# Three zero matmuls instead of one as fillers in each of the first twelve attention steps

## The chip, the cores and the metric

The kernel runs on one core of one Trainium2 chip. The metric is the device time of one execution in microseconds (us). In what follows PE is TensorE, DVE VectorE, ACT ScalarE, POOL GpSimd and SP SyncE, which issues the DMAs.

## The reference

The reference is a local attention followed by a gated layer. The batch is 4, there are 8 heads, 768 positions and 64 channels a head. A query sees the first 8 keys of the sequence (the global ones) and the 96 keys up to its own.

```python
scores = scale * np.matmul(q, k.transpose(0, 1, 3, 2))
...
scores = scores + bias[None, :, :, :]
scores = np.where(keep, scores, -1000000000.0)
scores = scores - np.max(scores, axis=-1, keepdims=True)
a = np.exp(scores)
a = a / (np.sum(a, axis=-1, keepdims=True) + 1e-09)
return np.matmul(a, v).astype(np.float32)
...
for k in range(K):
    gate_pre += conv_w[k][None, None, :] * xp[:, k:k + S, :]
gate = 1.0 / (1.0 + np.exp(-gate_pre))
val = x @ w_val
return (gate * val @ w_out).astype(np.float32)
```

The attention output x (512 channels) goes through a causal convolution of five taps, whose sigmoid gates the product of x with w_val. The gated value is multiplied with w_out.

## The kernel before

The work is cut into 32 groups (batch, half of the sequence, pair of heads), each of three steps, so 96 steps of 128 queries by two heads. What a step does, and on which engine:

- S (L406, PE): for a whole group at once, the scores of its three steps, twelve matmuls into four PSUM banks. The banks of one group are the only ones, so S of the next group waits until all bias passes of this one have read them.
- AM (L414, DVE): the bias pass, one for each head. It adds the bias to the scores, scales, and keeps the row minimum in `mins`. Tile t.
- EX (L424, ACT): the exponential with its sum `sm`. Then `sm` is guarded (L431, POOL or DVE), its reciprocal `rs` taken (L434, DVE) and the probabilities p multiplied by it (L439, POOL or DVE, two instructions a step).
- PT (L449, L452, L455, PE): transposes of p into the bank `pt`, of which there is one. EV (L149 on ACT, L151 on DVE) copies it to `a`.
- PV (L473, L477, L480, PE): once a group, the product with v into the bank `x`, of which there is one. Before it, four columns of history are put there (L548 a memset, or a copy).
- From x come xh (a rounded copy, L149 or L151), xl (the rest, L556, DVE) and the five taps of the convolution (the first L566 on ACT or L568 on DVE, the other four L564 on DVE). The bank is free for the next group when these are done.

Four groups make a phase, of which there are eight. For each phase a sigmoid on ACT (L599, with a table load before it and one behind it), 48 matmuls `val` (L606), the gating g = val times gate (L613, DVE), its split into gh and gl (L619, POOL or DVE), and 36 matmuls `o` (L626), whose result is copied (`ob`) and stored. The two banks of `val` and `o` take turns, so the second `o` of a phase waits for the g of the fourth `val`. The fourth `val` of phase 0 is val_0_3, its gated value g_0_3, its second output o_0_1.

At the start eight blocks of 64-bit weights, ('w', 0) to ('w', 7), are taken apart: an absolute value on ACT (L305), five passes on DVE (L313 to L325), a rounded copy (L149 on ACT or L151 on DVE) and two passes for the rest (L344, L348, POOL or DVE). The first four become wvh and wvl, the others woh and wol.

The order of the instructions on each engine is fixed when the program is built. Each operation is added to `Plan` with a due time, the engines that may do it and an assumed cost on each, and the operations that it follows. `Plan.order` (L80) goes through them as a list scheduler: it takes the engine that could start something first, and of what could start there, what is due first; where an operation may run on two engines, it takes the one that would end it first. A changed cost of one operation therefore moves others, on every engine. At run time each engine goes through its own list strictly in that order and waits by semaphores for data alone.

The fillers are matmuls of ones by ones, 128x512 in bfloat16, into the tile `warm` (`zeros`, L235 to L242), of which nothing is read. Eight stand at the program's start. One more operation F for each of the twelve steps of the first four groups (L245 to L248) issues `FILL_N` of them. In the plan F follows the bias pass of its step, but it reads nothing of that pass, so that on the chip it waits for nothing except its place in PE's list.

Of the kernel before, what the change touches and what calls it, by code (L numbers as in the profile page):

```python
# [16 lines left out]
WARM = 8  # L17
S_B, PT_B, X_B = 4, 1, 1
U_D1, RAW_B = -0.4, 4
FILL_N, FILL_TO, U_F = 1, 4, 0.2  # L20
W_AT = (0, 3, 6, 9, 14.5, 17, 22, 22.5)
SPARE = {"vector": 0.6, "gpsimd": -0.2, "scalar": 0.0}
XH_B, GATE_B, P_B, T_B, A_B, V_B, W_B, WT_B = 7, 2, 5, 8, 9, 4, 2, 1
# [874 lines left out]
```

## Time and profile before

| | us |
|---|---|
| three runs | 317.21, 318.02, 318.74 |
| median | 318.02 |
| the profiled execution, its time | 317.56 |
| its span, first to last instruction | 315.8 |
| PE busy in the span | 282.6 |
| DVE busy in the span | 230.2 |
| mean granted PE clock | 0.966 |

The profiled execution is 0.46 us below the median, and 1.76 us of its time lie outside the span. Times in the profile count from the span's start. A row of the list of instructions has the start, the duration, the engine and line, the operation, the tile written and those read, and in brackets the engine's idle time before it and what ended it. Durations of neighbours overlap by some 0.07 us, since an instruction starts before the one ahead has drained. A row of a table by stretches has the stretch, its length, and the busy time of each engine with its instructions. The granted clock is a share of TensorE's full clock.

### The profile page before, as it was taken

The numbers are of one execution on the slowest core, as the hardware profiler recorded it, in microseconds if no ns is written. First come the engines' busy times: TensorE is split into PE (matmuls) and PEld (weight loads), VectorE is DVE, ScalarE is ACT, GpSimd is POOL, SyncE is SP. The second block draws the span as 40 slices with busy tenths as digits, with TensorE's granted clock in tenths as the row PEclk, the third lists the DMA queues.
The fourth block names the chain that finished last, engine by engine and source line by source line (L and its number), as shares of the span: only waits on it lengthen the run. The fifth ranks groups of instructions, "written<-read, shape, count | busy, mean of one in ns | idle before, by whom it ended". The sixth has DMA issues, their size and how long they took to land.

```text
span 315.8 us, 6866 instructions
## 1 busy us (share of the span) xinstructions
PE 282.6 (89%) x2131; PEld 225.6 (71%) x2133; DVE 230.2 (73%) x807; ACT 230.0 (73%) x643; POOL 159.2 (50%) x338
## 2 busy tenths in 40 slices
PE   7487766697999999999999999999999999999992
PEld 2254555585788778887787777888788777888981
DVE  5899889999679676787766777978676767885410
ACT  2667677977789677977797769977895779785320
POOL 5977968586335353355426443554434542750220
PEclk9769799989999999999999999999999999999997
DMA  6768655203444435332450444323443221001102
GB/s 188 267 220 258 190 172 180 85 2 85 125 138 137 120 109 179 117 86 73 137 175 26 118 138 141 119 86 92 155 147 92 67 84 70 0 3 61 41 36 75
DMA packets 21069, 36.27 MB, mean 115 GB/s; under 512 B 2592, under 2 KB 12832, under 8 KB 21024
## 3 DMA queue, kind: packets, MB, share of 16 engines
q1 hardware_dynamic: 21024, 35.75, 36.4%
q8 instruction: 19, 0.31, 0.4%
q14 instruction: 26, 0.21, 0.2%
HBM read 29.45 MB, written 6.29 MB: 113 GB/s over the span
## 4 chain that ended last, share of the span: by engine, by line
PE 40%; DVE 29%; POOL 10%; ACT 8%; issue 5%; DMA 4%; SPq 1%; POOLq 0%; ACTq 0%
PE o L626 13%; DVE gate L564 12%; PE val L606 9%; DVE t L414 7%; POOL p L439 6%; PE x L477 5%; PE x L480 3%; DVE xl L556 3%; PE s L406 3%; PE pt L452 3%; ACT gate L566 3%; PE pt L455 2%; POOL sm L431 2%; ACT p L424 2%; DMA v<-in_v 2%
## 5 line engine op out<-in xcount | busy, mean ns | idle before, releaser
L424 ACT ACTIVATE p<-t,mins 128x232 f32<-128x232 f32 (+1 forms) x192 | 90.3, 472 | 22.2 <-DVE mins L414 17.1
L439 POOL TENSOR_SCALAR p<-p,rs 128x232 f32<-128x232 f32 (+1 forms) x179 | 84.9, 487 | 33.3 <-DVE rs L434 22.9
L564 DVE SCALAR_TENSOR_TENSOR gate<-x,cwt,gate 128x384 f32<-128x384 f32 x128 | 78.1, 610 | 7.8 <-ACT gate L566 7.4
L414 DVE CUSTOM_DVE_ANT_0 t<-s,bias 128x232 f32<-128x232 f32 (+1 forms) x192 | 67.4, 371 | 0.0
L431 POOL TENSOR_SCALAR sm<-sm 128x2 f32<-128x2 f32 x92 | 20.8, 226 | 84.6 <-ACT p L424 79.5
L149 ACT COPY a<-pt 128x464 f32<-128x464 f32 (+1 forms) x90 | 46.2, 513 | 18.5 <-PE pt L455 13.7
L606 PE MATMUL val<-xh,wvh 128*128 128x384 f32 x128 | 48.0, 375 | 2.5 <-DVE g L613 2.2
L406 PE MATMUL s<-rk,rq 64*128 64x232 f32 (+1 forms) x384 | 44.9, 360 | 4.0 <-DVE ('w', 0)_y L313 2.8
L606 PE MATMUL val<-xl,wvh 128*128 128x384 f32 x128 | 44.2, 346 | 1.2 <-DVE xl L556 1.2
L626 PE MATMUL o<-woh,gh 128*128 128x512 f32 x96 | 41.4, 432 | 3.3 <-DVE g L613 3.3
L606 PE MATMUL val<-xh,wvl 128*128 128x384 f32 x128 | 44.2, 346 | 0.0
L452 PE MATMUL pt<-ident,p 104*128 104x104 f32 x160 | 33.2, 276 | 11.7 <-ACT a L149 5.2
L452 PEld LDWEIGHTS pt<-ident,p 104*128 104x128 f32 x160 | 19.6, 141 | 31.9 <-POOL p L439 16.9
L434 DVE RECIPROCAL rs<-sm 128x2 f32<-128x2 f32 x96 | 15.6, 162 | 34.6 <-POOL sm L431 33.3
L406 PEld LDWEIGHTS s<-rk,rq 64*128 64x128 f32 x384 | 32.4, 186 | 11.2 <-DVE ('w', 0)_y L313 3.3
L626 PE MATMUL o<-wol,gh 128*128 128x512 f32 x96 | 37.9, 395 | 0.0
L626 PE MATMUL o<-woh,gl 128*128 128x512 f32 x96 | 37.8, 394 | 0.0
L424 ACT ACTIVATION_READ_ACCUMULATOR p<-t,mins 128x1 f32 x192 | 36.4, 190 | 0.0
L619 POOL TENSOR_TENSOR gl<-g,gh 128x384 fp32r<-128x384 f32 x27 | 27.7, 1026 | 16.3 <-ACT gh L149 15.1
L477 PE MATMUL x<-a,v 128*64 128x128 f32 x320 | 32.5, 281 | 0.3 <-ACT a L149 0.2
L455 PE MATMUL pt<-ident,p 128*128 128x128 f32 x160 | 31.4, 278 | 0.0
L606 PEld LDWEIGHTS val<-xh,wvh 128*128 128x128 f32 x128 | 24.8, 194 | 5.2 <-DVE g L613 3.8
(150 smaller groups left out, 465.9 us busy)
## 6 DMA issues: line engine op xcount, KB each, us to landing
rq<-in_qT SPq DMA_DIRECT2D x32, 192.0 KB, 3.6
v<-in_vw SPq DMA_DIRECT2D x16, 384.0 KB, 3.2
out<-ob SPq DMA_DIRECT2D x24, 256.0 KB, 2.1
v<-in_vw SPq DMA_DIRECT2D x16, 256.0 KB, 2.8
rk<-in_kT SPq DMA_DIRECT2D x16, 252.0 KB, 3.7
rk<-in_kT SPq DMA_DIRECT2D x16, 200.0 KB, 3.1
w<-in_wv SPq DMA_DIRECT2D x4, 512.0 KB, 4.6
w<-in_wo SPq DMA_DIRECT2D x4, 512.0 KB, 4.5
```

Source lines behind the costliest of these rows:

```text
L149: nc.scalar.copy(dst, src)
L406: nc.tensor.matmul(T["s", g, k, j][:, :n], T["rq", g][r, k * P : (k + 1) * P], T["rk", g][r, c0 : c0 + n], start=True, stop=True)
L414: nc.vector.tensor_tensor_reduce(out=t[:, :n], in0=T["s", s // HB, s % HB, j][:, :n], in1=bias[:, h, :P] if n == P else bias[:, h, P:], op ...
L424: nc.scalar.activation(T["p", s][:, j, :n], T["t", s, j][:, :n], AF.Exp, bias=mins[:, s, j : j + 1], scale=-1.0, accum_out=T["sm", s][:, j ...
L439: engine(e).tensor_scalar(out=pr, in0=pr, scalar1=rs, scalar2=1.0, op0=ALU.mult, op1=ALU.mult)
L452: nc.tensor.transpose(pt[:, j * QA : (j + 1) * QA], pr[:QA, j, :P], ident[:QA, :QA])
L455: nc.tensor.transpose(pt[:, c : c + P], pr[:, j, CA:], ident)
L477: nc.tensor.matmul(head(j, P), T["v", g][:, k, j, 1], a[:, 2 * QA + j * P : 2 * QA + (j + 1) * P], start=True, stop=False)
L564: nc.vector.scalar_tensor_tensor(out=gt, in0=src, scalar=w, in1=gt, op0=ALU.mult, op1=ALU.add)
L606: nc.tensor.matmul(T["val", ph, m], (wvh, wvh, wvl)[r][:, c, m * P : (m + 1) * P], (T["xh", g], T["xl", g], T["xh", g])[r], start=(c == 0 ...
L619: engine(e).tensor_sub(tile_of(("gl", ph, m), [P, HT], F32R, "gl", 5), T["g", ph, m], T["gh", ph, m])
L626: nc.tensor.matmul(T["o", ph, k], (T["gh", ph, c], T["gl", ph, c], T["gh", ph, c])[r][:, cols], (woh, woh, wol)[r][:, c], start=(c == 0 an ...
```

## The change

One number changes:

```diff
-FILL_N, FILL_TO, U_F = 1, 4, 0.2
+FILL_N, FILL_TO, U_F = 3, 4, 0.2
```

Each of the twelve F operations now issues three of the matmuls, 24 more in all. Its cost in the plan is `0.22 * FILL_N` and goes from 0.22 to 0.66 us, so the list scheduler sets the operations of the first groups in another order, on all engines. From PV of group 6 and the scores of group 8 on, the lists of both programs are the same. The listings below show three places ahead of that where they differ. A listing gives line, instruction, tile written and read, and size; the last number of a name is only the buffer's.

On PE, behind the transposes of step 5 (first row), before: the fillers, the scores of group 3, the transposes of step 6 and then PV of group 1.

```order
L455 MATMUL pt_405<-ident,p_338 128x128 x2
L239 LDWEIGHTS const-bfloat16-1.0
L239 MATMUL warm<-const-bfloat16-1.0 128x512
...
L406 MATMUL s_0_456<-rk_268,rq_276 128x128
...
L406 MATMUL s_3_459<-rk_268,rq_276 128x232
L449 MATMUL pt_480<-ident,p_400 128x128 x2
L473 MATMUL x_469<-a_347,v_1_151 64x128 x2
...
L480 MATMUL x_469<-a_423,v_158 64x104 x2
```

The same place now:

```order
L455 MATMUL pt_418<-ident,p_343 128x128 x2
L239 LDWEIGHTS const-bfloat16-1.0
L239 MATMUL warm<-const-bfloat16-1.0 128x512
...
L473 MATMUL x_464<-a_356,v_1_151 64x128 x2
...
L480 MATMUL x_464<-a_432,v_158 64x104 x2
L449 MATMUL pt_492<-ident,p_423 128x128 x2
...
L406 MATMUL s_0_513<-rk_274,rq_282 128x128
...
L406 MATMUL s_3_516<-rk_274,rq_282 128x232
```

PV of group 1 and the transposes of step 6 have moved ahead of the scores of group 3; the three fillers ahead of the scores are now six ahead of PV and three between step 6 and the scores.

On POOL, from the first rest pass of weight block 6 on, before. Here sm_877 is step 17, sm_908 step 18, sm_926 step 19 and sm_938 step 20.

```order
L344 TENSOR_TENSOR ('w', 6)_h<-('w', 6)_h,woh 128x512
L431 TENSOR_SCALAR sm_877<-sm_877 128x2
L348 TENSOR_TENSOR wol<-('w', 6)_h,('w', 6)_r 128x512
L439 TENSOR_SCALAR p_876<-p_876,rs_921 128x232 x2
L431 TENSOR_SCALAR sm_908<-sm_908 128x2
L431 TENSOR_SCALAR sm_926<-sm_926 128x2
L439 TENSOR_SCALAR p_907<-p_907,rs_950 128x232 x2
L431 TENSOR_SCALAR sm_938<-sm_938 128x2
L439 TENSOR_SCALAR p_937<-p_937,rs_978 128x232 x2
L619 TENSOR_TENSOR gl_2_1005<-g_2_940,gh_2_981 128x384
L344 TENSOR_TENSOR ('w', 7)_h<-('w', 7)_h,woh 128x512
L348 TENSOR_TENSOR wol<-('w', 7)_h,('w', 7)_r 128x512
```

And now, where sm_826 is step 16, sm_887 step 17, sm_913 step 18 and sm_932 step 19:

```order
L344 TENSOR_TENSOR ('w', 6)_h<-('w', 6)_h,woh 128x512
L431 TENSOR_SCALAR sm_826<-sm_826 128x2
L348 TENSOR_TENSOR wol<-('w', 6)_h,('w', 6)_r 128x512
L439 TENSOR_SCALAR p_825<-p_825,rs_908 128x232 x2
L431 TENSOR_SCALAR sm_887<-sm_887 128x2
L431 TENSOR_SCALAR sm_913<-sm_913 128x2
L619 TENSOR_TENSOR gl_0_946<-g_0_884,gh_0_920 128x384
L439 TENSOR_SCALAR p_886<-p_886,rs_949 128x232 x2
L439 TENSOR_SCALAR p_912<-p_912,rs_955 128x232 x2
L431 TENSOR_SCALAR sm_932<-sm_932 128x2
L619 TENSOR_TENSOR gl_1_988<-g_1_962,gh_1_975 128x384
L439 TENSOR_SCALAR p_931<-p_931,rs_994 128x232 x2
```

The splits gl_0_0 and gl_0_1 and the two passes of step 19 have come from DVE, and the rest passes of block 7 have gone to it.

On DVE, the rows from g_0_1 (first) on, before:

```order
L613 TENSOR_TENSOR g_1_934<-val_1_562,gate_380 128x384
L613 TENSOR_TENSOR g_2_940<-val_2_889,gate_380 128x384
L434 RECIPROCAL rs_950<-sm_908 128x2
L434 RECIPROCAL rs_957<-sm_926 128x2
L439 TENSOR_SCALAR p_925<-p_925,rs_957 128x232 x2
L619 TENSOR_TENSOR gl_1_969<-g_1_934,gh_1_948 128x384
L434 RECIPROCAL rs_978<-sm_938 128x2
L313 TENSOR_SCALAR ('w', 7)_y<-('w', 7)_y 128x512
...
L325 SCALAR_TENSOR_TENSOR ('w', 7)_r<-w_747,('w', 7)_y 128x512
L556 TENSOR_TENSOR xl_1027<-x_931,xh_1022 128x384
```

And now, where rs_994 is step 19:

```order
L613 TENSOR_TENSOR g_1_962<-val_1_678,gate_392 128x384
L414 ISA t_1_968,mins<-s_3_870,bias 128x232
L313 TENSOR_SCALAR ('w', 7)_y<-('w', 7)_y 128x512
L613 TENSOR_TENSOR g_2_985<-val_2_895,gate_392 128x384
L434 RECIPROCAL rs_994<-sm_932 128x2
...
L325 SCALAR_TENSOR_TENSOR ('w', 7)_r<-w_774,('w', 7)_y 128x512
L434 RECIPROCAL rs_1029<-sm_965 128x2
L344 TENSOR_TENSOR ('w', 7)_h<-('w', 7)_h,woh 128x512
L556 TENSOR_TENSOR xl_1048<-x_959,xh_1043 128x384
L348 TENSOR_TENSOR wol<-('w', 7)_h,('w', 7)_r 128x512
```

Other operations that change their engine: to DVE go the passes of p of steps 11 and 14, the copy a_15, the rounded copy of weight block 6, and gh_0_3 and gl_0_3; away from DVE go xh_4, a history copy of four columns and one pass of step 22.

## The prediction

> **What bounds the kernel now.** I read the page's sums first, then the table by stretches (length, then PE, PEld, DVE, ACT and POOL busy, the clock, DMA).
>
> ```profile
> PE 282.6 (89%) x2131; PEld 225.6 (71%) x2133; DVE 230.2 (73%) x807; ACT 230.0 (73%) x643; POOL 159.2 (50%) x338
> 24.00:44.00 20.00, 16.72 (x111) 11.62 (x112) 18.22 (x60) 13.83 (x42) 15.28 (x26) 0.91 0.65 197
> 44.00:60.00 16.00, 10.15 (x98) 7.76 (x98) 15.38 (x51) 14.01 (x36) 12.62 (x19) 1.00 0.54 173
> 60.00:76.00 16.00, 12.98 (x85) 10.71 (x85) 15.06 (x44) 12.16 (x36) 11.53 (x16) 0.89 0.18 54
> 80.00:280.00 200.00, 194.97 (x1555) 160.09 (x1557) 148.65 (x550) 161.50 (x459) 91.12 (x220) 1.00 0.35 108
> ```
>
> PE's 89% is a mean over two stages. From 80 us on PE is busy for 195 of 200 us and DVE for 149: PE is the bound. Ahead of that DVE is busy for 91, 96 and 94% of the stretches and PE for 84, 63 and 81%: DVE sets the pace and PE waits. PE's list shows the border (the second row is o_0_1, the third the scores of group 8):
>
> ```profile
> 61.84 0.44 PE L606 MATMUL val<-xh,wvh 128*128 128x384 f32 x1 [1.96 <-DVE g L613]
> 77.18 0.51 PE L626 MATMUL o<-woh,gh 128*128 128x512 f32 x1 [1.67 <-DVE g L613]
> 79.83 1.28 PE L406 MATMUL s<-rk,rq 64*128 64x128 f32 x12
> ```
>
> The last long wait is for g_0_3 on DVE. From the scores of group 8 on both programs have the same lists, so the 236 us behind them should shift as a block, and the change is worth what it moves the start of these scores.
>
> **The fillers.** PE's rows around some of the twelve places:
>
> ```profile
> 9.71 1.28 PE L406 MATMUL s<-rk,rq 64*128 64x128 f32 x12 [2.81 <-DVE ('w', 0)_y L313]
> ...
> 21.41 0.38 PE L239 MATMUL warm<-const-bfloat16-1.0 128*128 128x512 bf16 x1 [0.21 <-issue]
> 21.72 1.28 PE L406 MATMUL s<-rk,rq 64*128 64x128 f32 x12
> ...
> 26.29 0.81 PE L239 MATMUL warm<-const-bfloat16-1.0 128*128 128x512 bf16 x3
> ...
> 29.76 0.66 PE L406 MATMUL s<-rk,rq 64*128 64x232 f32 x2 [0.25 <-DVE mins L414]
> ```
>
> One filler alone is 0.38 us and three are 0.81, so each more costs (0.81 - 0.38) / 2 = 0.22; at half clock I allow 0.44. The 24 are 5.3 us of PE, at most 10.6. What hides them: the six more behind the first scores (1.3) lie in the wait of 2.81. The two behind step 1 and four behind step 3 delay the scores of group 2 by 0.9 to 1.8. These end at 21.72 + 1.28 = 23.0, and DVE first reads them here:
>
> ```profile
> 25.31 0.28 DVE L414 CUSTOM_DVE_ANT_0 t<-s,bias 128x128 f32<-128x128 f32 x1
> ...
> 30.74 0.06 DVE L548 MEMSET x<- 128x4 f32 x1
> ```
>
> That leaves 2.3 us. The six behind step 5 (1.3, from about 26.3) stand ahead of PV of group 1, which waits for the memset in the second row anyway (now due at some 30.0, as block 3 stands behind it). Then come PV (1.1), the transposes of step 6 (0.5), three fillers (0.65) and the scores of group 3, at about 32.2 to 33.5 where their last row ended at 30.4. DVE has the passes of block 3, xl_1 and a tap ahead of their first bias pass, some 4 us behind the memset, so 34. The nine around step 9 stand ahead of and behind transposes that wait for POOL. So I cost the fillers at nothing; without these waits they would cost 5.3.
>
> Now the clock, by windows of 2 us (PE busy, clock), and the wait behind the slow products:
>
> ```profile
> 12.00:14.00 2.00, 0.73 (x2) 0.50 0.29 102
> 36.00:38.00 2.00, 1.94 (x6) 0.50 0.50 190
> 64.00:66.00 2.00, 1.76 (x7) 0.56 0.00 0
> ...
> 65.87 0.44 PE L606 MATMUL val<-xh,wvh 128*128 128x384 f32 x1 [0.23 <-DVE g L613]
> ```
>
> It is at or near half in three stretches. In the first two DVE is the later engine, and even behind the third PE waits 0.23 us more for DVE, so a full clock would be worth 0.3 at most; I take 0. The Trainium skill, "TensorE: Matmul & The Clock Gate", Part 1, says that the gate opens after a window of some 3.4 us of activity and closes after an idle one; by that rule the fillers would keep it open, and the sum would be 0.3 lower. That the clock falls where PE is idle agrees (0.73 of 2 us busy in the first row); that fillers hold it, no row shows.
>
> **DVE's work until g_0_3.** Rows for the prices, of which I take off 0.07 each for the overlap:
>
> ```profile
> 64.31 0.72 DVE L619 TENSOR_TENSOR gl<-g,gh 128x384 fp32r<-128x384 f32 x1
> 66.58 0.99 DVE L439 TENSOR_SCALAR p<-p,rs 128x232 f32<-128x232 f32 x2
> 13.43 0.67 DVE L344 TENSOR_TENSOR ('w', 0)_h<-('w', 0)_h,wvh 128x512 f32<-128x512 f32 x1
> 58.62 0.55 DVE L151 CAST xh<-x 128x384 fp32r<-128x384 f32 x1
> L151 DVE COPY a<-pt 128x464 f32<-128x464 f32 x3 | 1.9, 642 | 0.4
> L414 DVE CUSTOM_DVE_ANT_0 t<-s,bias 128x232 f32<-128x232 f32 (+1 forms) x192 | 67.4, 371 | 0.0
> ```
>
> To DVE come the passes of steps 11 and 14 (four at 0.47: 1.9), the rest passes of block 7 (1.2), a_15 (0.55) and the copy of block 6 (0.4, an estimate below xh's 0.48); one bias pass more stands ahead of g_0_3 (0.3). Away go the passes of step 19 (0.95), gl_0_0 and gl_0_1 (1.25), xh_4 (0.5) and the history copy (0.1). That is 4.35 - 2.8 = 1.55 more.
>
> Against it stand DVE's waits, and three rows for what follows:
>
> ```profile
> 35.90 0.17 DVE L434 RECIPROCAL rs<-sm 128x2 f32<-128x2 f32 x1 [0.35 <-POOL sm L431]
> 35.98 1.90 DVE L564 SCALAR_TENSOR_TENSOR gate<-x,cwt,gate 128x384 f32<-128x384 f32 x3
> 38.23 0.17 DVE L434 RECIPROCAL rs<-sm 128x2 f32<-128x2 f32 x1 [0.35 <-POOL sm L431]
> ...
> 43.18 0.62 DVE L564 SCALAR_TENSOR_TENSOR gate<-x,cwt,gate 128x384 f32<-128x384 f32 x1 [0.65 <-ACT gate L566]
> ...
> 57.43 0.41 DVE L322 TENSOR_SCALAR ('w', 6)_y<-('w', 6)_h 128x512 int32<-128x512 int32 x1
> ...
> 70.17 1.11 DVE L322 TENSOR_SCALAR ('w', 7)_y<-('w', 7)_h 128x512 int32<-128x512 int32 x1
> ...
> 73.13 0.62 DVE L564 SCALAR_TENSOR_TENSOR gate<-x,cwt,gate 128x384 f32<-128x384 f32 x1 [0.65 <-ACT gate L566]
> ```
>
> The four waits are 2.0. Now the reciprocals of steps 9 and 10 have taps and bias passes ahead of them, and behind xl_2 and xl_5 stands other work ahead of the tap that waited for ACT. I let all four go. Two come. Behind xl_1 the tap follows at once, which waits for ACT's first tap as at 43.18: 0.6. And rs of step 19 waits for POOL, which from the copy of block 6 on has two rest passes, four guards, gl_0_0 and three pairs of p ahead of it:
>
> ```profile
> 61.69 1.29 POOL L344 TENSOR_TENSOR ('w', 6)_h<-('w', 6)_h,woh 128x512 f32<-128x512 f32 x1 [2.65 <-issue]
> 63.06 0.19 POOL L431 TENSOR_SCALAR sm<-sm 128x2 f32<-128x2 f32 x1
> 64.60 1.20 POOL L439 TENSOR_SCALAR p<-p,rs 128x232 f32<-128x232 f32 x2
> 66.53 0.91 POOL L439 TENSOR_SCALAR p<-p,rs 128x232 f32<-128x232 f32 x2 [0.18 <-DVE rs L434]
> 69.57 1.43 POOL L619 TENSOR_TENSOR gl<-g,gh 128x384 fp32r<-128x384 f32 x1
> 77.77 1.01 POOL L619 TENSOR_TENSOR gl<-g,gh 128x384 fp32r<-128x384 f32 x1
> ```
>
> That is 2 x 1.29 + 4 x 0.19 + 1.01 + 3 x 0.91 = 7.1, beside 6.6 of DVE from the same copy on (four taps at 0.55, 2.2; three g and xl_4 priced as xh, 1.9; six bias passes, 1.8; reciprocals and a pass of block 7, 0.7). DVE waits 0.5.
>
> DVE's sum is then 1.55 + 0.6 + 0.5 - 2.0 = +0.65, if all else takes as long as before. But the pass of block 7 at 70.17 took 0.7 longer than that of block 6, the three taps 0.3 longer than three at 0.55, and besides the waits the stretches from 24 to 76 us hold 1.78 + 0.62 + 0.94 - 2.0 = 1.3 of small gaps, of which I count 0.9: 1.9 in all that another order may not have. DVE's end lies between +0.65 and -1.25. No row decides; I take the middle, -0.3.
>
> **PE behind g_0_3.** Before, the transposes of step 21 stand behind o_0_1; now ahead of it, in the wait:
>
> ```profile
> 77.99 0.34 PE L452 MATMUL pt<-ident,p 104*128 104x104 f32 x2
> ...
> 78.48 0.44 PE L477 MATMUL x<-a,v 128*64 128x128 f32 x4
> ```
>
> From 77.99 to 78.48 that takes 0.5 off the path. The sum is -0.3 - 0.5 = -0.8. Against the profiled execution's 317.56 that is 316.8; the median of the runs shown is 0.46 higher, so I give 317.2.
>
> **The rivals.** A difference below 0.5% (1.6 us: 316.4 to 319.6) a measurement of this kernel can hardly tell from none.
>
> - *Neither slow instructions nor new waits*: DVE at -1.25 and PE's 0.5 give -1.75; without the two new waits (1.1) -2.85. That is 316.3 to 315.2, and I name 315.7. For it: the long instructions look like chance meetings. Against: with more on DVE there is more to meet. 0.33.
> - *Nothing*: the waits come back elsewhere in the same size, 318.0. For it: DVE at 91 to 96% has little to gain. 0.10.
> - *POOL takes DVE's place between 59 and 70 us*, slower: its idle 2.65 us are used up by what comes to it. If gl takes 1.43 instead of 1.01 and the pairs of p 1.20 instead of 0.91, 1.3 more in all, rs of step 19 waits 1.8 and all of block 7 behind it; and where POOL is late, its two waits of 0.35 stay. 1.55 + 0.6 + 1.8 - 1.3 - 0.5 = +2.15, 320.2. It decides once DVE waits over 1.5 us at that reciprocal. 0.16.
> - *The fillers stay on the path*: each delays a score or transpose that DVE waits for, 24 x 0.22 = +5.3, 323.3. The waits above speak against it. 0.06. The Trainium skill, "TensorE: Matmul & The Clock Gate", Part 2, says that matmuls stay in program order, so that none behind a filler can pass it; the rows show none that does.
>
> **How the numbers follow.** The forecast has 0.35, with 316.3 to 318.2 of its own (sums of -1.75 and +0.15). Faster by over 0.5%: 0.33. Within: 0.35 + 0.10 = 0.45. Slower: 0.16 + 0.06 = 0.22. The range reaches to the far end of the first rival and just over the third: 315.0 to 320.4; the last rival and some of each tail are left out.
>
> **What would show it.** Right: g_0_3 ends 0.3 us earlier and the scores of group 8 start 0.8 earlier, at about 79.0; DVE waits some 0.5 at rs of step 19 and 0.6 at the first tap of group 1, and no more at steps 9 and 10 and behind xl_2 and xl_5; the scores of group 3 run without a break. Wrong: DVE under 90% busy between 24 and 76 us, bias passes that wait for scores, a wait for POOL of over 1.5, or a stage behind the scores of group 8 that differs by more than 0.5 from the 236 us of before.

## The result, and the profile after

The changed kernel takes 322.80 us (median of 4 runs, 321.56 to 323.85) against 318.22 of the kernel before: ratio 1.0148, 95% interval 1.011 to 1.0186. It is slower by 4.6 us, where 0.8 faster was forecast, and lies outside the range. The profiled execution took 322.73 us, its span is 321.0.

PE's list of after, at the fillers and at the border between the two stages:

```profile
7.13 3.56 PE L239 MATMUL warm<-const-bfloat16-1.0 128*128 128x512 bf16 x9
10.63 1.28 PE L406 MATMUL s<-rk,rq 64*128 64x128 f32 x12
...
20.95 2.77 PE L239 MATMUL warm<-const-bfloat16-1.0 128*128 128x512 bf16 x6
23.64 1.31 PE L406 MATMUL s<-rk,rq 64*128 64x128 f32 x12
...
29.95 0.44 PE L473 MATMUL x<-a,v 128*64 128x128 f32 x4 [1.82 <-DVE x L548]
...
32.14 1.28 PE L406 MATMUL s<-rk,rq 64*128 64x128 f32 x12
...
81.63 0.69 PE L626 MATMUL o<-woh,gh 128*128 128x512 f32 x1
...
85.44 1.28 PE L406 MATMUL s<-rk,rq 64*128 64x128 f32 x12
```

The last row is the scores of group 8: 5.61 later than before (79.83). Behind them 321.0 - 85.44 = 235.6 us are left, 236.0 before. So all of the loss lies ahead of 85 us. The scores of group 2 (23.64) start 1.92 later than before, a little more than the forecast of 0.9 to 1.8; they end at 23.64 + 1.31 = 24.95, still ahead of DVE's first read of them (26.13). PV of group 1 and the scores of group 3 (32.14) are not later than forecast, though the fillers are there.

DVE's list of after: the first bias pass of group 2, the tap behind xl_1, the p passes of steps 11 and 14, the rest passes of block 7, and g_0_3.

```profile
26.13 0.28 DVE L414 CUSTOM_DVE_ANT_0 t<-s,bias 128x128 f32<-128x128 f32 x1
...
34.99 0.62 DVE L564 SCALAR_TENSOR_TENSOR gate<-x,cwt,gate 128x384 f32<-128x384 f32 x1 [0.71 <-ACT gate L566]
...
42.19 2.60 DVE L439 TENSOR_SCALAR p<-p,rs 128x232 f32<-128x232 f32 x2
...
52.58 2.60 DVE L439 TENSOR_SCALAR p<-p,rs 128x232 f32<-128x232 f32 x2
...
74.64 1.42 DVE L344 TENSOR_TENSOR ('w', 7)_h<-('w', 7)_h,woh 128x512 f32<-128x512 f32 x1
...
76.45 0.90 DVE L348 TENSOR_TENSOR wol<-('w', 7)_h,('w', 7)_r 128x512 fp32r<-128x512 f32 x1
...
81.03 0.55 DVE L613 TENSOR_TENSOR g<-val,gate 128x384 f32<-128x384 f32 x1
```

What POOL did at those times:

```profile
42.04 1.27 POOL L344 TENSOR_TENSOR ('w', 4)_h<-('w', 4)_h,woh 128x512 f32<-128x512 f32 x1
43.39 1.26 POOL L348 TENSOR_TENSOR wol<-('w', 4)_h,('w', 4)_r 128x512 fp32r<-128x512 f32 x1
...
52.43 1.28 POOL L344 TENSOR_TENSOR ('w', 5)_h<-('w', 5)_h,woh 128x512 f32<-128x512 f32 x1
53.78 1.27 POOL L348 TENSOR_TENSOR wol<-('w', 5)_h,('w', 5)_r 128x512 fp32r<-128x512 f32 x1
...
74.04 1.46 POOL L619 TENSOR_TENSOR gl<-g,gh 128x384 fp32r<-128x384 f32 x1
75.48 1.33 POOL L439 TENSOR_SCALAR p<-p,rs 128x232 f32<-128x232 f32 x2
```

A pair of p passes, priced at 0.94, took 2.60: each pair starts 0.15 behind the start of POOL's first rest pass (42.04) and ends just behind the end of the second (43.39 + 1.26 = 44.65, and the pair ends at 44.79). DVE waits for no semaphore there, so the view of waits doesn't show it; it shows only as long instructions. g_0_3 starts at 81.03, 4.46 later than before:

```profile
76.57 0.55 DVE L613 TENSOR_TENSOR g<-val,gate 128x384 f32<-128x384 f32 x1
```

The other 5.61 - 4.46 = 1.15 arise on PE between g_0_3 and the scores of group 8. The table by stretches of after:

```profile
44.00:60.00 16.00, 9.83 (x66) 7.79 (x66) 15.78 (x47) 10.03 (x29) 7.56 (x13) 0.83 0.45 159
...
80.00:84.00 4.00, 3.21 (x17) 2.06 (x19) 3.00 (x12) 2.28 (x9) 2.82 (x7) 0.72 0.00 0
84.00:284.00 200.00, 195.42 (x1558) 160.74 (x1555) 147.51 (x545) 160.36 (x455) 89.81 (x218) 1.00 0.36 108
```

From 44 to 60 us DVE is busy for 99% (15.78 of 16, before 15.38), and yet fewer of its instructions fall into the stretch (47 instead of 51); ACT falls from 14.01 to 10.03. From 80 to 84 us, between g_0_3 and the scores of group 8, the granted clock is 0.72.

### The profile page after: what moved, and what is told of

It reads as the page before. It is cut to its first block, busy times and chain, and to the rows that moved or that the text cites. A ratio compares the mean times of both kernels' runs of the same rounds, so it can differ in the third digit from the quotient of the medians.

```text
span 321.0 us, 6913 instructions
## 1 busy us (share of the span) xinstructions
PE 291.6 (91%) x2154; PEld 229.8 (72%) x2157; DVE 234.5 (73%) x810; ACT 229.6 (72%) x642; POOL 155.8 (49%) x336
## 4 chain that ended last, share of the span: by engine, by line
PE 43%; DVE 28%; POOL 9%; ACT 8%; issue 6%; DMA 3%; SPq 1%; POOLq 0%; ACTq 0%
PE o L626 13%; DVE gate L564 12%; PE val L606 8%; DVE t L414 6%; POOL p L439 6%; PE x L477 6%; PE s L406 4%; PE x L480 4%; DVE xl L556 3%; PE pt L452 3%; PE pt L455 3%; ACT gate L566 2%; DMA w<-in_wv 2%; ACT xh L149 1%; ACT p L424 1%
## 5 line engine op out<-in xcount | busy, mean ns | idle before, releaser
L431 POOL TENSOR_SCALAR sm<-sm 128x2 f32<-128x2 f32 x92 | 19.9, 217 | 93.9 <-ACT p L424 88.9
L149 ACT COPY a<-pt 128x464 f32<-128x464 f32 (+1 forms) x89 | 45.5, 512 | 16.9 <-PE pt L455 14.4
L606 PE MATMUL val<-xh,wvh 128*128 128x384 f32 x128 | 47.0, 367 | 0.2
L452 PE MATMUL pt<-ident,p 104*128 104x104 f32 x160 | 34.1, 278 | 12.4 <-POOL p L439 8.0
L606 PE MATMUL val<-xh,wvl 128*128 128x384 f32 x128 | 43.5, 340 | 0.0
L619 POOL TENSOR_TENSOR gl<-g,gh 128x384 fp32r<-128x384 f32 x28 | 28.7, 1024 | 16.6 <-ACT gh L149 15.1
L477 PE MATMUL x<-a,v 128*64 128x128 f32 x320 | 33.9, 292 | 0.3 <-ACT a L149 0.2
L556 DVE TENSOR_TENSOR xl<-x,xh 128x384 fp32r<-128x384 f32 x32 | 17.7, 554 | 16.1 <-ACT gate L566 10.0
```

Source lines behind the costliest of these rows:

```text
L149: nc.scalar.copy(dst, src)
L452: nc.tensor.transpose(pt[:, j * QA : (j + 1) * QA], pr[:QA, j, :P], ident[:QA, :QA])
L477: nc.tensor.matmul(head(j, P), T["v", g][:, k, j, 1], a[:, 2 * QA + j * P : 2 * QA + (j + 1) * P], start=True, stop=False)
L606: nc.tensor.matmul(T["val", ph, m], (wvh, wvh, wvl)[r][:, c, m * P : (m + 1) * P], (T["xh", g], T["xl", g], T["xh", g])[r], start=(c == 0 ...
L619: engine(e).tensor_sub(tile_of(("gl", ph, m), [P, HT], F32R, "gl", 5), T["g", ph, m], T["gh", ph, m])
```

## The experiments

**Theory 1, meetings**: the plan, which now counts 0.66 for each place of the fillers, gave the p passes of steps 11 and 14 to DVE; POOL, free of them, starts its rest passes (L344, L348) at that very moment, and DVE's passes wait for whole POOL instructions. **Rival 1**: the 24 fillers themselves lie on PE's path (5.3 us). **Rival 2**: the new order on PE (scores of group 3 behind PV of group 1) makes the loss.

Ratios are to the kernel before, measured beside it on the same chip, with 95% intervals. That kernel's own median was between 317.8 and 318.9 there, so rows are compared by their ratios:

| kernel | median us | ratio (interval) |
|---|---|---|
| after | 322.80 | 1.0148 (1.011 to 1.0186) |
| three fillers, order of before | 317.75 | 1.0004 (0.9984 to 1.0025) |
| one filler, order of after | 323.12 | 1.0150 (1.0118 to 1.0182) |
| after, p passes of steps 11, 14 on POOL | 318.62 | 1.0014 (0.9991 to 1.0037) |
| after, rest passes of blocks 4, 5 later | 317.86 | 1.0003 (0.9979 to 1.0027) |
| the same, and block 7's rest passes on POOL | 317.77 | 0.9964 (0.9948 to 0.9980) |
| after, only block 7's rest passes on POOL | 322.59 | 1.0127 (1.0107 to 1.0147) |
| before, p passes of step 14 on DVE | 323.98 | 1.0169 (1.0146 to 1.0193) |
| the same, rest passes of block 5 later | 319.52 | 1.0017 (0.9995 to 1.0040) |
| the same, and two DVE copies more | 321.69 | 1.0124 (1.0096 to 1.0153) |
| the same, and four | 323.59 | 1.0192 (1.0172 to 1.0211) |

### Fillers or order

The cost that the plan counts and the number that is issued are taken apart. Three fillers in the order of before (on after's text):

```diff
-            plan.add(("F", 3 * g + i), 3 * g + i + U_F, {PE: 0.22 * FILL_N}, lambda e: zeros(FILL_N),
+            plan.add(("F", 3 * g + i), 3 * g + i + U_F, {PE: 0.22}, lambda e: zeros(FILL_N),
```

> The order of before on all engines, with three fillers issued at each of the twelve places (the plan still counts one). Theory 1, meetings of DVE's passes with POOL's rest passes, which come from the new order alone: 318.2, within 1 us of before, since the 24 more fillers lie in PE's waits. Rival 1, the fillers themselves on PE's path: 24 x 0.22 = 5.3 us more than before, some 323. Rival 2, the new order on PE (scores of group 3 behind PV of group 1): 318.2 too, so this run decides between the fillers and the order only.

One filler in the order of after (on before's text):

```diff
-            plan.add(("F", 3 * g + i), 3 * g + i + U_F, {PE: 0.22 * FILL_N}, lambda e: zeros(FILL_N),
+            plan.add(("F", 3 * g + i), 3 * g + i + U_F, {PE: 0.66}, lambda e: zeros(FILL_N),
```

> The order of after on all engines, but one filler issued at each place (the plan still counts three). Theory 1: 322 to 323, as after, since the loss is in the order. Rival 1, the fillers on PE's path: 318.2, as before. Rival 2, the new order on PE: 322 to 323.

Measured: 1.0004 and 1.0150. The 24 matmuls cost nothing that can be told from zero (at most 0.25%, 0.8 us, by the interval), and the order costs everything: rival 1 falls. Its price had come out right (323.3 forecast, 322.80 measured), which shows how little an agreeing total says of the cause.

### The meetings undone

Here and below the planned list is edited before it is issued: move(key, e, behind, first) gives an operation to engine e, puts it behind another, and lets POOL copy one column of a tile ahead of it (read), so that it starts only when that tile has been written. First, the p passes go to POOL, ahead of the rest passes:

```diff
+        for s, i in ((11, 4), (14, 5)):
+            for j in range(2):
+                move(("NM", s, j), e=POOL)
+            move(("WS", i), behind=("NM", s, 1))
```

> After, but the p passes of steps 11 and 14 are done by POOL, ahead of its rest passes of blocks 4 and 5; all else stands as in after. Theory 1: each pair took DVE 2.60 us (as long as POOL's two rest passes beside it), so 5.2 us of DVE go, and 317.6 to 319.5 is left, the upper end if POOL's later passes or other meetings give some back. Rivals 1 and 2 (fillers, order on PE): both are left as they are, 322 to 323.

Second, the passes stay on DVE, and only the moment is changed at which POOL starts its rest passes:

```diff
+        move(("WS", 4), behind=("W1", 5), first=lambda: read(T[("w", 5), "y"][:, :1]))
+        move(("WP", 4), behind=("WS", 4))
+        move(("WS", 5), behind=("NM", 14, 1), first=lambda: read(T["p", 14][:, 1, :1]))
```

> After, with the p passes of steps 11 and 14 left on DVE, but POOL starts its rest passes of block 4 only behind DVE's second pass over block 5, and those of block 5 only behind the p passes of step 14 (a POOL copy of one column that reads what these wrote stands ahead of them). Theory 1: a pair of p then takes 0.94 on DVE instead of 2.60, so 2 x 1.66 = 3.3 us go: 319 to 320.5. Rivals 1 and 2: 322 to 323. If the two passes are slow by themselves, without POOL beside them, 322 to 323 as well, with 2.60 in both pairs.

Measured: 318.62 and 317.86. The second run removes nothing from DVE, POOL or PE and adds two small copies; yet it takes back the whole loss, and ends 1.1 us below the range expected. DVE's list of that run (all lines are one further down in its text):

```profile
42.06 0.59 DVE L440 TENSOR_SCALAR p<-p,rs 128x232 f32<-128x232 f32 x2
...
50.71 0.59 DVE L440 TENSOR_SCALAR p<-p,rs 128x232 f32<-128x232 f32 x2
...
76.92 0.55 DVE L614 TENSOR_TENSOR g<-val,gate 128x384 f32<-128x384 f32 x1
```

PE's row of the scores of group 8, and the stretch that ends there, at full clock:

```profile
79.78 1.28 PE L407 MATMUL s<-rk,rq 64*128 64x128 f32 x12
...
76.00:80.00 4.00, 3.31 (x35) 2.36 (x36) 2.90 (x12) 2.29 (x9) 2.92 (x7) 1.00 0.00 0
```

A pair by itself takes 0.59, so one meeting costs 2.60 - 0.59 = 2.01 and two cost 4.02; g_0_3 comes 81.03 - 76.92 = 4.11 earlier. Theory 1 holds, and rival 2 falls: PE's order is that of after here too. Two things that the expectation left out bring the time below its range: the pair was 0.35 cheaper than my 0.94 (0.7 for both), and PE runs at full clock behind g_0_3 (the scores of group 8 come 85.44 - 79.78 = 5.66 earlier, g_0_3 only 4.11). The profiled execution, at 317.03, is 0.8 below the median, so these two need not add up to what the medians show.

### The meeting by itself

A small kernel, which leaves the computation out, runs four instructions of DVE or POOL by themselves, then four of each engine at once; each writes tiles of its own, and where both run the same operation, both read one common operand. DVE and POOL wait for each other between the groups.

> A small kernel of its own that leaves the computation out: four DVE or POOL instructions by themselves, then the same beside four of the other engine, on tiles of their own. Theory 1, a DVE pass over SBUF alone waits for POOL's whole instruction: a p pass of 128x232 takes 0.3 to 0.5 alone and about 1.3 beside POOL's differences of 128x512, which take 1.27; a DVE difference of 128x512 does the same; a tap of 128x384 that reads PSUM takes 0.6 alone and beside them. The Trainium skill, SBUF - State Buffer, section on SBUF's two separate sides, says that DVE and GpSimd have a shared pair of ports as an exclusive lock, for the whole instruction; by that page it comes out so. Rival: the two slow passes of 2.60 came from something else, and each pass takes beside POOL within 0.1 of what it takes alone.

In this first form the instructions did not stay in the order of the text, so that groups meant to run alone ran beside others; it settles nothing. The second form keeps the order:

```diff
+    with tc.manual_schedule():
...
+        for j in range(4):
+            G.tensor_sub(h[:, j], h[:, j], hx)
+        for j in range(4):
+            V.tensor_scalar(out=p[:, j], in0=p[:, j], scalar1=r, scalar2=1.0, op0=ALU.mult, op1=ALU.mult)
```

> The small kernel again, which leaves the computation out, now with its instructions kept in the order of the text: each group of four by itself first, then the pairs. Theory 1: p passes of 128x232 on DVE 0.3 alone and beside POOL's p passes 0.3 to 0.6, but some 1.3 each beside POOL's differences of 128x512 (1.27 each); DVE's differences of 128x512 0.68 alone and 1.3 to 1.7 beside POOL's; taps of 128x384 that read PSUM 0.61 alone and beside them. Rival: no pass takes over 0.1 more beside POOL than alone.

DVE's list: each operation alone (L84 p passes, L93 differences, L96 taps), then beside POOL's differences (L101, L111, L116), and p passes beside POOL's p passes (L106):

```profile
13.58 1.08 DVE L84 TENSOR_SCALAR p<-p,rs 128x232 f32<-128x232 f32 x4
...
22.10 2.49 DVE L93 TENSOR_TENSOR hh<-hh,hx 128x512 f32<-128x512 f32 x4
...
25.07 2.18 DVE L96 SCALAR_TENSOR_TENSOR gate<-x,rs,gate 128x384 f32<-128x384 f32 x4
...
27.73 5.02 DVE L101 TENSOR_SCALAR p<-p,rs 128x232 f32<-128x232 f32 x4
...
33.24 1.81 DVE L106 TENSOR_SCALAR p<-p,rs 128x232 f32<-128x232 f32 x4
...
35.53 6.66 DVE L111 TENSOR_TENSOR hh<-hh,hx 128x512 f32<-128x512 f32 x4
...
42.67 2.18 DVE L116 SCALAR_TENSOR_TENSOR gate<-x,rs,gate 128x384 f32<-128x384 f32 x4
```

Four p passes take 1.08 alone and 5.02 beside POOL's four differences, as long as these (5.0); beside POOL's p passes 1.81. Differences go from 2.49 to 6.66. Taps, which read PSUM, take 2.18 both times. The Trainium skill, "SBUF — State Buffer", section on SBUF's two separate sides, says that DVE and GpSimd have one pair of SBUF ports in common, which one instruction holds from its start to its end while the other blocks fully, and that a DVE instruction takes part in it in a two-port mode or with two inputs in SBUF. DVE's times agree for the differences, with two inputs in SBUF (6.66), and for the taps, with one input in SBUF (2.18); for the p passes (5.02) they agree if these run in a two-port mode, which no run here shows.

### Block 7's rest passes

In after DVE does them (1.42 and 0.90, beside POOL's gl and p). They go back to POOL, with and without the delay of blocks 4 and 5:

```diff
+        move(("WS", 7), e=POOL, behind=("NM", 20, 1))
+        move(("WP", 7), e=POOL, behind=("WS", 7))
```

> The kernel with POOL's rest passes of blocks 4 and 5 started later, and the two rest passes of block 7, which the new order gave to DVE, back on POOL behind the p passes of step 20. On DVE these two took 1.42 and 0.91 us, beside POOL's gl and p. Theory 1 (DVE's time until g_0_3 sets the end): 2.3 us less than the kernel without the second edit (317.9), so 315.6, less than before. Rival: by then PE or POOL's later guards are what is late, and it stays at 317 to 318.

> After, with only the two rest passes of block 7 back on POOL behind the p passes of step 20; the p passes of steps 11 and 14 stay on DVE beside POOL's rest passes. Theory 1: 2.3 us less than after, 320.5. Rival: the loss is all in the two meetings at steps 11 and 14, and it stays at 322 to 323.

Measured: 0.9964 with the delay (1.0003 without this edit, so 1.2 us less where 2.3 were expected; the two intervals just touch), and 1.0127 alone (1.0148 for after; the intervals overlap). Theory 1 had the price too high, and the rival of the first run was half right. In the profiled execution of the second run DVE's pair of step 14 began 0.07 ahead of POOL's first rest pass and took 1.61 instead of 2.60, so what a meeting costs also depends on who comes first.

DVE's list of the first run, with the delay, tells where the rest went:

```profile
76.16 0.17 DVE L435 RECIPROCAL rs<-sm 128x2 f32<-128x2 f32 x1 [1.38 <-POOL sm L432]
```

POOL has the two rest passes ahead of the guard of the next step, so DVE now waits 1.38 there. Still, this first version is faster than before by 0.36%, the only one whose interval lies below 1; it is less than the 0.5% that the prediction set as the bound.

### The same meeting in the order of before

Before's order with one filler, but the p passes of step 14 given to DVE, first so that they meet the rest passes of block 5, then with these delayed:

```diff
+        for j in range(2):
+            move(("NM", 14, j), e=DVE, behind=("NM", 14, 0) if j else ("RC", 14))
```

> Before, with one filler and its own order, but DVE does the p passes of step 14 behind their reciprocal; so POOL is free for its rest passes of block 5 at once, and both run together. Theory 1: the pair takes 2.60 us on DVE as in after, and the end comes 2.0 to 2.6 later, 320.2 to 320.8. Rival (the order on PE or the fillers make the loss): neither is touched, 318.2 to 318.8.

```diff
+        move(("WS", 5), first=lambda: read(T["p", 14][:, 1, :1]))
```

> As the kernel before it in this call (before, with the p passes of step 14 on DVE), but POOL starts the rest passes of block 5 only when these p passes have ended (a copy of one column of them stands ahead). Theory 1: the pair takes 0.59 us, and the end is at 318.2 to 318.8, 2.0 less than without the delay. Rival: no difference between the two.

Measured: 323.98 and 319.52. The passes take 2.59 and 0.59 us, as expected, but both times lie above what was expected (320.2 to 320.8 and 318.2 to 318.8), and between the two the end moves by 4.5 for 2.0 of DVE. To see whether the meeting does harm beside DVE's time, the delayed version got copies from PSUM into a tile that nobody reads (four, then two, behind the p passes):

```diff
+                nc.vector.tensor_copy(tile_of(("spin",), [P, HT], F32, "spin", 1), T["x", 3][:, HIST:])
```

> As the kernel with the p passes of step 14 on DVE and POOL's rest passes of block 5 behind them (319.5, 1.0017 of before), and four more DVE copies of 128x384 from PSUM into a tile that nobody reads, right behind these p passes: some 2 us of DVE, as much as the meeting cost there (2.59 instead of 0.59), but without POOL. The meeting moved the median by 4.5. Theory 1, completed: a delay of DVE at this place costs more than itself because PE, which waits longer, then runs longer at half clock, whatever the delay is made of: 323 to 324.5 (1.014 to 1.018). Rival: the meeting does harm beside DVE's own time, through POOL; then the copies cost their 2 us and no more, 321 to 322.

> The same with two copies, some 1 us. Theory 1, completed: 1 to 2.3 us above the kernel without copies, 320.5 to 322. Rival: 320.5.

Measured: 1.0192 and 1.0124, against 1.0017 without copies: 5.6 us for four copies (2.32 in the trace) and 3.4 for two (1.14). The copies are more than a delay of DVE, though. By the profile ACT's first tap, which reads the same tile x, waited for them, and xl on DVE then waited for this tap, here with two copies (lines are one further down in these kernels too):

```profile
52.04 0.58 ACT L567 ACTIVATE gate<-x,cwt 128x384 f32<-128x384 f32 x1 [3.58 <-DVE spin L719]
...
52.65 0.56 DVE L557 TENSOR_TENSOR xl<-x,xh 128x384 fp32r<-128x384 f32 x1 [0.65 <-ACT gate L567]
```

With four copies the wait is 0.65 too. So DVE is held up for 1.14 + 0.65 = 1.8 and 2.32 + 0.65 = 3.0, and each us of it costs 1.9; the meeting costs 4.5 for 2.0, or 2.2. Each of these differences is uncertain by about 1 us, so the two prices can't be told apart. What is shown is that DVE's time at this place counts about double, with a meeting and without one. Whether ACT's lateness has a share in the price of the copies, and whether the meeting does some smaller harm besides, stays open. PE's list with two copies shows a part of how it doubles:

```profile
53.27 0.44 PE L607 MATMUL val<-xl,wvh 128*128 128x384 f32 x1 [3.60 <-DVE xl L557]
...
56.96 0.69 PE L478 MATMUL x<-a,v 128*64 128x128 f32 x4
...
59.47 2.23 PE L407 MATMUL s<-rk,rq 64*128 64x232 f32 x12
```

and its table by stretches the clock (the sixth column behind the length):

```profile
52.00:56.00 4.00, 2.02 (x10) 1.47 (x10) 3.35 (x12) 3.75 (x10) 2.56 (x3) 0.79 0.49 189
56.00:60.00 4.00, 4.00 (x30) 3.40 (x32) 3.85 (x14) 3.88 (x8) 2.91 (x6) 0.50 0.01 2
```

The same places in before:

```profile
51.55 0.44 PE L606 MATMUL val<-xl,wvh 128*128 128x384 f32 x1 [1.19 <-DVE xl L556]
...
54.89 0.44 PE L477 MATMUL x<-a,v 128*64 128x128 f32 x4
...
56.52 1.45 PE L406 MATMUL s<-rk,rq 64*128 64x232 f32 x12
...
56.00:60.00 4.00, 3.10 (x28) 2.22 (x28) 3.85 (x10) 3.97 (x4) 2.58 (x5) 1.00 0.45 124
```

PE waits 3.60 instead of 1.19; behind that the clock is 0.50 from 56 to 60 us, where it was 1.00, and PV with the scores of group 5 takes 59.47 + 2.23 - 56.96 = 4.74 instead of 56.52 + 1.45 - 54.89 = 3.08. So 1.7 us come on top of the delay against before. But the version without copies has the low clock in its profiled execution too, behind a shorter wait:

```profile
52.91 0.44 PE L607 MATMUL val<-xl,wvh 128*128 128x384 f32 x1 [1.82 <-DVE xl L557]
...
56.00:60.00 4.00, 4.00 (x32) 3.38 (x34) 3.85 (x14) 3.92 (x8) 3.07 (x5) 0.50 0.01 2
```

That execution is the slowest of its twelve (321.06; the fastest took 317.79). So the slow clock behind a wait of PE is seen, but that the longer wait makes it fall is not shown, and no run held the clock up there.

## Why the prediction was wrong, point by point

- **The border and the block behind it**: right. 235.6 us stand behind the scores of group 8, 236.0 before.
- **The fillers at nothing**: right. 1.0004 with three of them in the old order; PV of group 1 started at 29.95 (forecast 30.0), the scores of group 3 at 32.14 (32.2 to 33.5), and DVE waited for the scores of neither group 2 nor group 3.
- **The clock at 0**: it held for the fillers by themselves, where the interval leaves room for the 0.3 either way. With three in the old order the profiled execution has a clock of 1.00 from 24 to 44 us, where before had 0.91, and the time is the same. Whether the fillers held it there is not settled: the run with the p passes on POOL, with three fillers too, has 0.91. The 0 was wrong for the sum: behind DVE's delay the clock was 0.72 at 80 to 84 us, and 1.00 up to the same scores in the run with later rest passes, which has the same fillers and the same order on PE.
- **DVE's work until g_0_3**: here the prediction failed, in the terms "the passes of steps 11 and 14 (four at 0.47: 1.9)" and "the rest passes of block 7 (1.2)". The mechanism of the sum was right, the prices were not: 2 x 2.60 = 5.2 and 1.42 + 0.90 = 2.3. With these the forecast of -0.3 becomes -0.3 + 3.3 + 1.1 = +4.1, and +4.46 was measured; that the two come so close is partly luck, as the next two points show. I had taken 0.99 for a pair from a place where POOL ran p passes too (four beside p passes take 1.81, beside differences 5.02), and did not ask what POOL would run beside them at their new place. A row of before had the answer, a single p pass of DVE:

```profile
22.77 1.15 DVE L439 TENSOR_SCALAR p<-p,rs 128x232 f32<-128x232 f32 x1
```

with this on POOL:

```profile
22.33 1.45 POOL L348 TENSOR_TENSOR wvl<-('w', 1)_h,('w', 1)_r 128x512 fp32r<-128x512 f32 x1
```

- **Waits**: the four old ones went, as forecast, and the tap behind xl_1 waited 0.71 (0.6). The 0.5 at the reciprocal of step 19 did not come; with later rest passes, where DVE gets there sooner, it did (0.60). Four that I had not forecast came in after (0.46, 0.28, 0.57 and 0.28), the last of them a bias pass that waits for scores, one of my signs of being wrong. In all DVE waited 2.3, where 1.1 was forecast and 2.0 stood before.
- **The "slow instructions"**: I counted 1.9 us of them, small gaps included, as chance that might not recur, took off half, 0.95, and gave the case without them 0.33. With all that moved taken at its measured price less 0.07 an instruction (+5.9) and the waits (+0.3), the 4.46 leave -1.7 for the rest of DVE's list: it did run shorter, by nearly all of the 1.9. But larger ones of the same kind came with the passes that moved. One of the old ones fits a meeting: the pass of block 7 at 70.17, 1.11 long, lay beside POOL's gl, which ended at 69.57 + 1.43 = 71.00. That each of them was one was not tried.
- **PE behind g_0_3, -0.5**: right at full clock: from g_0_3 to the scores of group 8 before took 79.83 - 76.57 = 3.26, the run with later rest passes 79.78 - 76.92 = 2.86. In after it took 85.44 - 81.03 = 4.41, at a clock of 0.72.
- **The rivals**: none was it. "POOL takes DVE's place" had the sign and the engine, but through a wait at a reciprocal that did not come; its 320.2 had room for POOL's instructions to stretch, but not for DVE's.

## What to carry to other kernels

An elementwise pass has no price of its own where DVE and POOL both work in SBUF: before a pass is moved to DVE, look at what POOL will run at that moment, all the more as POOL is free for it because the pass left. Look for such meetings among long instructions, not among waits. And a plan that prices engines one by one can make a loss out of a change of 0.44 us on another engine: test the order apart from the work.

## What was not expected of the hardware

- In the small kernel's groups by line, POOL's four differences stand alone (L87), beside p passes (L99), beside DVE's differences (L109) and beside taps (L114):

```profile
L109 POOL TENSOR_TENSOR h<-h,hx 128x512 f32<-128x512 f32 x4 | 6.3, 1595 | 0.0
...
L99 POOL TENSOR_TENSOR h<-h,hx 128x512 f32<-128x512 f32 x4 | 5.0, 1290 | 0.0
...
L114 POOL TENSOR_TENSOR h<-h,hx 128x512 f32<-128x512 f32 x4 | 4.9, 1265 | 0.0
L87 POOL TENSOR_TENSOR h<-h,hx 128x512 f32<-128x512 f32 x4 | 4.9, 1263 | 0.0
```

  Beside p passes only DVE pays (5.02 instead of 1.08, POOL 5.0 instead of 4.9); beside DVE's differences both pay (6.66 instead of 2.49, and 6.3 instead of 4.9).
- Copies that hold DVE up for 1.8 us, the wait behind them included, cost 3.4, and 3.0 cost 5.6, at a place where PE waits for DVE. In the profiled execution with two copies the clock is 0.50 for 4 us behind that wait.
